# Four f chunks of the first two batches moved from twelve plain products into two seven-product pairs, with the loads of batches 1 to 3 reordered

## The chip, the core and the metric

The kernel runs on one core of a Trainium2 chip. The metric is device time in microseconds (us) of one execution. A core has a matrix engine (TensorE, PE in the profile; its weight loads are PEld), a vector engine (VectorE, DVE), a scalar engine (ScalarE, ACT), GpSimd (POOL, which here issues the input loads) and SyncE (SP, which issues the transposing DMAs and the stores). Each engine runs its own instructions in the order of the program and waits on semaphores. The matrix engine writes PSUM, which has eight banks; vector and scalar engine read it.

## What is computed

```python
# per batch b of 8 and head h of 12, sequence 448, head size 64
scores = q @ k.T / 8 - log(448)
attn   = sigmoid(scores)            # not a softmax
x      = concat_heads(attn @ v)     # 3584 tokens x 768
gate   = relu(x @ w_gate)           # w_gate, w_val: 768 x 1536
val    = x @ w_val
out    = (gate * val) @ w_out       # w_out: 1536 x 768
```

All products run in float16 with float32 accumulation.

## The kernel before

**Attention.** For each batch there are 21 score units: three groups g of four heads, seven chunks c each. A unit (`qk_unit`, L292) is four matmuls into two PSUM banks and two sigmoids on the scalar engine. `pv_group` (L300) then multiplies a whole group with v, 28 matmuls into two banks, and the vector engine scales the result into the tile `xT` (L184). Queries and keys must be transposed first. For batches 0 and 1 the matrix engine does that (`pe_transposes`, L195). From batch 2 on `dma_transposes` (L211) copies a group of k and q into the tile `rel` on the vector engine (L215) and SP issues one transposing DMA (L219).

**The feed-forward part.** Its unit is an f chunk, 128 of the 1536 columns of `w_gate` and `w_val`. For batches 0 and 1 it is done plainly by `gv` (L304): six gate matmuls and six value matmuls, a relu, a multiplication into `hT` (L327). Batch 0 is done in two halves of 256 and 192 tokens, batch 1 in one piece of 448. From batch 2 on two batches form a group, and `gv_pair` (L506) does two f chunks of both batches. There the two-by-two block product (gate and value columns against the two halves of the model dimension) is done in seven block products in place of eight, 42 matmuls of 448 columns. It needs sums of weight blocks (`gate_sums` L477 and `unit_sums` L481) and sums of activation blocks (`batch_sums` L500), all on the vector engine. The output product is done the same way for two token tiles (`down_pair` L423, after `token_sums` L409 and `weight_sums` L392, the latter four sums of blocks of `wo`); one token tile per group is done plainly (`down` L341, items "t").

**Order.** The program is written out by hand. The plain chunks stand in a queue; `ffn_mix` (L574) pops some of them and runs hooks at given places. Pairs, token tiles and output pairs stand in `work` (L659) and are taken by `next_work` (L675), which calls `prepare` for the next item's sums and runs a list of jobs beside its matmuls. Each batch is cut into stretches of score units (`cuts`), and after each stretch m come `mix[m]` plain chunks or one item of `work`. In batch 1 the mix is 3, 3, 3, 3, 3, 2, in batch 2 it is 2, 2, 1, 1, 1, 2 and then output pair 0 of group 0, in batch 3 it is 1, 1, 1 and then two items.

**PSUM.** `bank` (L76) hands out the eight banks in turn; a new tile waits for the readers of the last tile in its bank.

**Loads.** All input loads are issued by POOL, eight in flight. Through L160 they are issued as early as the queue allows: batch 0, the gate and value weights in five pieces, batch 1 between them. Those of batch 2 follow in batch 1. `hold(b, g)` (L645) is a copy of two elements on POOL out of a transposed tile: POOL issues nothing more until that transposing DMA has landed. In batch 1's last stretch `late_loads` (L652) holds for group 1 of batch 2, then loads v of batch 2 and `wo`; k, q and v of batch 3 follow in the first stretch of batch 2.

Of the kernel before, what the change touches and what calls it, by code (L numbers as in the profile page):

```python
# [17 lines left out]
def kernel(  # L18
# [10 lines left out]
    nc = tc.nc  # L29
# [6 lines left out]
    NCH = S // 64  # L36
    NDC = DM // P
    NFC = DF // P
    TW = 2 * NCH
    QCUT = 4  # L40
    HALVES = ((0, QCUT), (QCUT, NCH))
# [12 lines left out]
    PTp = ctx.enter_context(tc.tile_pool(name="PTp", bufs=11))  # L54
    xTp = ctx.enter_context(tc.tile_pool(name="xTp", bufs=3))
    hTp = ctx.enter_context(tc.tile_pool(name="hTp", bufs=1))
    ysbp = ctx.enter_context(tc.tile_pool(name="ysbp", bufs=4))
    gsbp = ctx.enter_context(tc.tile_pool(name="gsbp", bufs=6))
    first_sbuf = ExitStack()
    early = first_sbuf.enter_context(tc.tile_pool(name="early", bufs=1))  # L60
# [83 lines left out]
    def load_gv(f0, f1, which=(0, 1)):  # L144
        fs = slice(f0 * P, f1 * P)
        for i in which:
            wt, src = ((wg, moe_w_gate), (wv, moe_w_val))[i]
            nc.gpsimd.dma_start(wt[:, :, fs], src[:, fs].rearrange("(c p) f -> p c f", p=P))
# [4 lines left out]
    load_gv(2, 4)  # L153
    load_gv(4, 6)
    load(1, 0, 1, "kq")
    load_gv(6, 9)
    load(1, 1, 2, "kq")
    load_gv(9, 12)
    load_v(1)
    load(1, 2, 3, "kq")  # L160

# [206 lines left out]
    def open_late():  # L368
        first_sbuf.close()
        pool = ctx.enter_context(tc.tile_pool(name="late", bufs=1))  # L370
        late["T"] = pool.tile([P, 4, HF, HM], FP16, tag="T", name="T")
        late["X"] = pool.tile([P, 3, HD, S], FP16, tag="X", name="X")
        late["sums"] = ctx.enter_context(tc.tile_pool(name="sums", bufs=2))

    def sub(o, a, b):
        nc.vector.tensor_tensor(out=o, in0=a, in1=b, op=AOP.subtract)
# [114 lines left out]
    def batch_blocks(g, ks):  # L491
        x1, x2 = xT_tiles[2 * g], xT_tiles[2 * g + 1]
        lo, hi = slice(*ks), slice(HD + ks[0], HD + ks[1])
        return [late["X"][:, i, lo] for i in range(3)] + [x1[:, lo], x1[:, hi], x2[:, lo], x2[:, hi]]

    def batch_sums_t1(g):
        T1, _, _, B11, _, B12, _ = batch_blocks(g, (0, HD))
        sub(T1, B12, B11)

    def batch_sums(g, ks):  # L500
        T1, T2, T4, _, B21, B12, B22 = batch_blocks(g, ks)
        sub(B12, B22, B12)
        sub(T2, B22, T1)
        sub(T4, B21, T2)

    def gv_pair(g, f, beside, first_copy):  # L506
        x1, x2 = xT_tiles[2 * g], xT_tiles[2 * g + 1]
        T1, T2, T4 = (late["X"][:, i] for i in range(3))
        B11, B21, T3, B22 = x1[:, 0:HD], x1[:, HD:NDC], x2[:, 0:HD], x2[:, HD:NDC]
        b, c, a = ([bank(nm) for _ in range(2)] for nm in ("u", "g2", "g1"))  # L510
        later((6, 7, 4, 5, 2, 3))
        gs = [[gsbp.tile([P, S], FP32, tag="gsb", name="gsb") for _ in range(3)] for _ in range(2)]
        if g not in hT_tiles:
            hT_tiles[g] = hTp.tile([P, NFC, 2 * S], FP16, tag="hT", name="hT")
        h = hT_tiles[g]
        sets = []
        for u in range(2):
            us, fs = slice(u * P, (u + 1) * P), slice((f + u) * P, (f + u + 1) * P)
            S1, S2, S4 = (t[:, :, us] for t in sums[("w", g, f)])
            sets.append((  # L520
                wg[:, 0:HD, fs], wg[:, HD:NDC, fs], wv[:, HD:NDC, fs],
                S1, S2, wv[:, 0:HD, fs], S4,
            ))
        del sums[("w", g, f)]

        def product(ps, i, W, first=True):
            for u in range(2):
                products([(ps[u], S, HD, sets[u][i], W, first)])

        def copy(i, ps, by=nc.scalar.copy):  # L530
            for u in range(2):
                by(gs[u][i][:], ps[u][:, 0:S])  # L532

        def plus(i, ps):
            for u in range(2):
                nc.vector.tensor_tensor(  # L536
                    out=gs[u][i][:], in0=ps[u][:, 0:S], in1=gs[u][i][:], op=AOP.add
                )

        def gated(u, o, gate_sb, val):  # L540
            nc.vector.scalar_tensor_tensor(
                out=h[:, f + u, o : o + S], in0=gate_sb, scalar=0.0, in1=val, op0=AOP.max, op1=AOP.mult
            )

        product(b, 0, B11)
        copy(0, b, first_copy)
        product(c, 3, T1)
        copy(2, c)
        product(b, 4, T2, False)
        copy(1, b)  # L550
        beside()
        product(a, 1, B21)
        plus(0, a)
        product(b, 5, T3, False)
        plus(2, b)
        product(c, 6, B22, False)
        plus(1, c)
        product(b, 2, T4, False)
        for u in range(2):
            gated(u, 0, gs[u][0][:], b[u][:, 0:S])  # L560
        for u in range(2):
            gated(u, S, gs[u][1][:], gs[u][2][:])
# [7 lines left out]
    def push_first(half, fs, act_relu=True):  # L570
        c0, c1 = HALVES[half]
        push_gv(0, 64 * c0, 64 * (c1 - c0), fs, act_relu)
# [53 lines left out]
            if (i, u) in after:  # L626
                after[(i, u)]()
    slots[5].pv()
    push_first(1, range(0, 6))
    for f0 in range(6, 12, 2):  # L630
        for half in range(2):
            push_first(half, range(f0, f0 + 2))


    order = [(g, c) for g in range(NG) for c in range(NCH)]
# [1 line left out]
    def pv_finish(b):  # L637
        pv_group(b, NG - 1)
        if b < 2:
            push_gv(b, 0, S, range(NFC))  # L640

    first_psum.close()
    open_banks("ring1")
# [4 lines left out]
    def both(b, g):  # L648
        pe_transposes(b, g, 0)
        pe_transposes(b, g, 1)  # L650

    def late_loads():  # L652
        dma_transposes(2, 1)
        hold(2, 1)
        load_v(2)
        load_o()


    work = deque()  # L659

    def push_group(g):
        tail = [("t", g, 6)] + [("y", g, p) for p in range(3)]
        if g == 0:
            tail.insert(0, tail.pop(1))
        work.extend([("w", g, f) for f in range(0, NFC, 2) if g > 0] + tail)

    def prepare():
        if work:
# [6 lines left out]
    def next_work(jobs=(), alone=False, first_act=False):  # L675
        kind, g, i = work.popleft()

        def beside():
            for job in jobs:
                job()  # L680

        if kind == "y":
            down_pair(g, i, beside, prepare, not work, scaled_act if alone or first_act else scaled)
        elif kind == "w":
            gv_pair(g, i, lambda: (prepare(), beside()), nc.scalar.copy if alone else nc.vector.tensor_copy)
        else:
            beside()
            prepare()
            down(g, i)

    ffn_mix(1, [(1, lambda: both(1, 0))])
    for b in range(1, B):
# [6 lines left out]
        count = len(cuts) - 1  # L699
        hooks = {}  # L700
        if b == 1:
            mix = (3, 3, 3, 3, 3, 2)
            hooks = {
                1: [(1, lambda: both(1, 1))],
                3: [(1, lambda: both(1, 2))],
                4: [(3, lambda: dma_transposes(2, 0))],
                5: [(2, late_loads)],
            }
        elif b == 2:
            mix = (2, 2, 1, 1, 1, 2)  # L710
            hooks = {
                2: [(0, prepare)],
                4: [(0, lambda: weight_sums(0))],
                5: [(1, lambda: weight_sums(1)), (0, lambda: weight_sums(2))],
            }
            open_late()
        elif b == 3:
            mix = (1, 1, 1, 0, 0)
        else:
            mix = (0,) * count  # L720
        for m in range(count):
            jobs = []
            for i, (g, c) in enumerate(order[cuts[m] : cuts[m + 1]]):
# [7 lines left out]
                    else:  # L731
                        pv_group(b, pv_at[m][0])
                qk_unit(b, g, c)
            if m == 0 and b > 1:
                jobs.append(lambda: dma_transposes(b, 2))
            if b == 2 and m == count - 1:
                jobs.append(lambda: (dma_transposes(3, 0), dma_transposes(3, 1)))
            elif b == 3 and m == count - 1:
                jobs.append(lambda: (dma_transposes(4, 0), dma_transposes(4, 1)))
            elif 0 <= m - count + 2 and 3 < b < B - 1:  # L740
                jobs.append(lambda: dma_transposes(b + 1, m - count + 2))
            if b == 1:
                if m == 0:
                    load(2, 0, 1, "kq")
                    load(2, 1, 2, "kq")
                    load(2, 2, 3, "kq")
            elif m == 0 and b + 1 < B:
                if b == 3:
                    jobs.append(lambda: hold(3, 2))
                jobs.append(lambda: (load(b + 1, 0, 3, "kq"), load_v(b + 1)))  # L750
# [4 lines left out]
                jobs.append(lambda: batch_sums(b // 2 - 1, (1, HD)))  # L755
            if b == 2 and m == count - 1:
                ffn_mix(mix[m], hooks[m])
                next_work(jobs + [lambda: weight_sums(3)], first_act=True)
            elif mix[m]:
                for job in jobs:  # L760
                    job()
                ffn_mix(mix[m], hooks.get(m, ()))
            else:
                next_work(jobs)
            if b == 3 and m in (1, 3):
                for f in range(*((0, 8, 2), (8, NFC, 2))[m // 2]):
                    gate_sums(f, f + 2)
    pv_finish(B - 1)
    push_group(B // 2 - 1)
# [33 lines left out]
```

## Time and profile before

| what | value |
|---|---|
| three runs | 398.97, 397.96, 398.85 us; median 398.85 |
| the profiled execution | 399.14 us |
| its span, first to last instruction | 397.3 us |
| mean granted TensorE clock | 1.000 |
| from the first score unit of batch 1 to the last product before batch 2 | 33.83 to 64.25 us |
| batch 2, up to the first score unit of batch 3 | 64.25 to 101.36 us |
| engines busy in 33.83 to 64.25 (30.42 us) | PE 29.58, DVE 11.31, ACT 23.45 |
| engines busy in 64.25 to 101.30 (37.05 us) | PE 36.66, DVE 20.12, ACT 25.13 |

A timeline line gives the start in us, the stretch that the merged instructions cover, the engine, the line of the kernel, the operation, the tile written and the tiles read, the shape and the count; square brackets hold the idle time of the engine before them and what ended it. Instructions overlap at their ends. So the distance between two starts tells what one costs its engine, and the duration tells how long its result takes. DMA lines give the kilobytes written and the time from issue to landing.

### The profile page before, as it was taken

The numbers are of one execution on the slowest core, as the hardware profiler recorded it, in microseconds if no ns is written. First come the engines' busy times: TensorE is split into PE (matmuls) and PEld (weight loads), VectorE is DVE, ScalarE is ACT, GpSimd is POOL, SyncE is SP. The second block draws the span as 40 slices with busy tenths as digits, with TensorE's granted clock in tenths as the row PEclk, the third lists the DMA queues.
The fourth block names the chain that finished last, engine by engine and source line by source line (L and its number), as shares of the span: only waits on it lengthen the run. The fifth ranks groups of instructions, "written<-read, shape, count | busy, mean of one in ns | idle before, by whom it ended". The sixth has DMA issues, their size and how long they took to land.

```text
span 397.3 us, 8744 instructions
## 1 busy us (share of the span) xinstructions
PE 388.5 (98%) x3488; PEld 217.5 (55%) x3488; DVE 279.6 (70%) x539; ACT 223.2 (56%) x476; POOL 49.5 (12%) x73
## 2 busy tenths in 40 slices
PE   8999999999999999999999999999999999999995
PEld 3678686445455554554555555455455555555563
DVE  3453345358377889999758889999776779987662
ACT  5946768684785565655665455565566233543121
POOL 8643400700030300003000300000000000000000
PEclk9999999999999999999999999999999999999999
DMA  9999994999999893224945695222013320000135
GB/s 150 196 198 204 206 129 87 180 203 190 203 143 180 167 218 53 46 48 54 177 84 133 130 219 89 48 21 57 19 40 81 81 79 2 0 1 2 40 94 146
DMA packets 68953, 43.69 MB, mean 110 GB/s; under 512 B 35888, under 2 KB 65584, under 8 KB 68912
## 3 DMA queue, kind: packets, MB, share of 16 engines
q0 software_dynamic: 30736, 23.33, 39.2%
q1 hardware_dynamic: 37744, 19.34, 23.2%
q8 instruction: 27, 0.44, 0.4%
q10 hardware_dynamic: 432, 0.46, 0.4%
q14 instruction: 14, 0.11, 0.1%
HBM read 47.19 MB, written 11.01 MB: 146 GB/s over the span
## 4 chain that ended last, share of the span: by engine, by line
PE 84%; DMA 11%; POOL 2%; ACT 1%; issue 0%; DVE 0%; ACTq 0%; POOLq 0%; DVEq 0%
PE u L385 32%; PE g L385 15%; PE y L385 8%; PE qk_ps L232 7%; PE pv_ps L250 7%; PE g_ps L309 5%; PE v_ps L309 5%; DMA wg<-in_moe_w_gate_dram 4%; DMA v<-in_v_dram 3%; PE ya L346 3%; DMA q<-in_q_dram 2%; PE yb L346 1%; DMA qkT<-rel 1%; ACT PT L187 1%; POOL k L110 1%; POOL q L110 1%
## 5 line engine op out<-in xcount | busy, mean ns | idle before, releaser
L187 ACT ACTIVATE PT<-qk_ps 128x448 f16<-128x448 f32 (+3 forms) x318 | 150.5, 595 | 72.6 <-PE qk_ps L232 72.5
L385 PEld LDWEIGHTS <-S 128*128 128x128 f16 x540 | 52.8, 98 | 43.6
L536 DVE TENSOR_TENSOR gsb<-g,gsb 128x448 f32<-128x448 f32 x72 | 42.9, 625 | 14.6 <-PE g L385 14.1
L232 PE MATMUL qk_ps<-qkT 64*64 64x448 f16 (+2 forms) x756 | 49.9, 336 | 1.3 <-DVE qkT L206 0.5
L421 ACT ACTIVATE ysb<-u 128x384 f32<-128x384 f32 x27 | 13.4, 498 | 53.4 <-PE u L385 53.4
L327 DVE TENSOR_TENSOR hT<-gate_sb,v_ps 128x256 f16<-128x256 f32 (+2 forms) x36 | 16.2, 465 | 34.7 <-ACT gate_sb L318 22.3
L532 ACT COPY gsb<-u 128x448 f32<-128x448 f32 x48 | 25.7, 566 | 23.9 <-PE u L385 22.9
L250 PE MATMUL pv_ps<-PT,v 64*64 64x448 f16 (+2 forms) x756 | 37.7, 329 | 1.1 <-DMA v<-in_v_dram 0.8
L184 DVE TENSOR_SCALAR xT<-pv_ps 128x448 f16<-128x448 f32 (+2 forms) x53 | 27.9, 567 | 15.2 <-PE pv_ps L250 13.8
L385 PEld LDWEIGHTS <-hT 128*128 128x128 f16 x288 | 27.7, 98 | 19.8 <-issue 2.1
L232 PEld LDWEIGHTS <-qkT 64*64 64x64 f16 x756 | 20.0, 105 | 25.5 <-issue 16.3
L309 PE MATMUL v_ps<-xT,wv 128*128 128x256 f16 (+2 forms) x216 | 33.3, 290 | 0.3 <-DMA wv<-in_moe_w_val_dram 0.3
L309 PE MATMUL g_ps<-xT,wg 128*128 128x256 f16 (+2 forms) x216 | 33.5, 291 | 0.1
L385 PEld LDWEIGHTS <-wv 128*128 128x128 f16 x216 | 21.1, 98 | 19.7
L385 PEld LDWEIGHTS <-wg 128*128 128x128 f16 x216 | 20.3, 98 | 20.6 <-issue 3.0
L250 PEld LDWEIGHTS <-v 64*64 64x64 f16 x756 | 21.8, 107 | 12.8 <-DMA v<-in_v_dram 1.5
L385 PE MATMUL u<-T,hT 128*128 128x384 f16 x144 | 27.3, 326 | 0.0
L437 DVE SCALAR_TENSOR_TENSOR ysb<-y,ysb 128x384 f32<-128x384 f32 x24 | 13.4, 557 | 17.8 <-PE y L385 10.3
L309 PEld LDWEIGHTS <-wg 128*128 128x128 f16 x216 | 18.5, 98 | 11.5 <-issue 5.0
L110 POOL DMA_DIRECT2D k<-in_k_dram x14 | 10.9, 780 | 110.7 <-DVE rel L215 104.4
L309 PEld LDWEIGHTS <-wv 128*128 128x128 f16 x216 | 20.1, 98 | 7.9 <-DMA wv<-in_moe_w_val_dram 0.6
L385 PE MATMUL u<-xT,wg 128*128 128x448 f16 x108 | 23.5, 353 | 0.1
(69 smaller groups left out, 531.0 us busy)
## 6 DMA issues: line engine op xcount, KB each, us to landing
out_dram<-ysb SPq DMA_DIRECT2D x52, 192.0 KB, 3.0
k<-in_k_dram POOLq DMA_DIRECT2D x5, 672.0 KB, 11.7
q<-in_q_dram POOLq DMA_DIRECT2D x5, 672.0 KB, 14.9
v<-in_v_dram POOLq DMA_DIRECT2D x8, 336.0 KB, 15.4
v<-in_v_dram POOLq DMA_DIRECT2D x16, 168.0 KB, 15.2
k<-in_k_dram POOLq DMA_DIRECT2D x8, 224.0 KB, 10.4
wo<-in_moe_w_out_dram POOLq DMA_DIRECT2D x1, 1536.0 KB, 13.1
q<-in_q_dram POOLq DMA_DIRECT2D x6, 224.0 KB, 11.3
```

Source lines behind the costliest of these rows:

```text
L110: nc.gpsimd.dma_start(t16[:, xs, cs], rows_of(src, b)[:, xs, cs])
L184: nc.vector.tensor_scalar(out=xT, in0=src, scalar1=XSCALE, scalar2=None, op0=AOP.mult)
L187: nc.scalar.activation(PT_ap, ps_ap, AF.Sigmoid, bias=sig_bias, scale=qk_scale)
L232: nc.tensor.matmul(out_of(hh)[o : o + 64, :], qkT[rows, c, cols], qkT[rows, NCH + c0 : NCH + c1, cols], start=True, stop=True, tile_positi ...
L250: nc.tensor.matmul(ps[hh][64 * r : 64 * r + 64, 0:qn], v16[rows, 2 * g + hh, c * D : (c + 1) * D], pieces[c][rows, hh, :], start=(c == 0), ...
L309: nc.tensor.matmul(ps[-1][:, 0:qn], wt[:, dc, f * P : (f + 1) * P], xT_tiles[b][:, dc, q0 : q0 + qn], start=(dc == 0), stop=(dc == NDC - 1),)
L327: nc.vector.tensor_tensor(out=hT_tiles[g][:, f, o : o + qn], in0=gate_sb[:, 0:qn], in1=ps[1][:, 0:qn], op=AOP.mult,)
L346: nc.tensor.matmul(ps[:, 0 : m1 - m0], hT_tiles[g][:, f, t * P : (t + 1) * P], wo[:, f, m0:m1], start=(f == 0), stop=(f == NFC - 1),)
L385: nc.tensor.matmul(ps[:, 0:n], A[:, k_, :], W[:, k_, :], start=(first and k_ == 0), stop=(k_ == kn - 1), skip_group_check=True,)
L421: nc.scalar.activation(o, ps[:, 0:HM], AF.Copy, scale=OUT_SCALE)
L532: by(gs[u][i][:], ps[u][:, 0:S])
L536: nc.vector.tensor_tensor(out=gs[u][i][:], in0=ps[u][:, 0:S], in1=gs[u][i][:], op=AOP.add)
```

## The change

The last four f chunks (8 to 11) of batches 0 and 1 are no longer done by `gv`. They become two items "w" of `work` for group 0 (pair 8 and pair 10 below), done by `gv_pair` in batch 2 after the stretches m = 1 and m = 2. The constant `PAIR0 = 8` marks the first of them. A fourth activation sum gets a block of its own in the late tile `X` for group 0, since the plain chunks of batch 1 still read the block that the later groups overwrite. The buffers for output rows go from four to three. The relu of all plain chunks of batch 0 moves to the vector engine.

The mix of plain chunks becomes 2, 1, 2, 1, 2, 1 in batch 1 and 3, 0, 0, 1, 1, 0 in batch 2; a 0 takes an item of `work`, so batch 2 has pair 8, pair 10 and, after its last stretch, output pair 0. That output pair's first copy moves from the scalar to the vector engine. Its fourth weight sum, which stood beside its products, stands before them.

The weights of chunks 8 to 11 are loaded after a hold on the transposing DMA of batch 2's group 0 (`second_loads`), and ahead of the rest of batch 2's k, q and v. `wo` and batch 3's k and q come after a hold on batch 2's group 2 (`late_loads`), batch 3's v after a hold on batch 3's group 1.

```diff
...
-    ysbp = ctx.enter_context(tc.tile_pool(name="ysbp", bufs=4))
+    ysbp = ctx.enter_context(tc.tile_pool(name="ysbp", bufs=3))
...
     load(1, 0, 1, "kq")
-    load_gv(6, 9)
+    load_gv(6, 8)
     load(1, 1, 2, "kq")
-    load_gv(9, 12)
     load_v(1)
     load(1, 2, 3, "kq")
...
-        late["X"] = pool.tile([P, 3, HD, S], FP16, tag="X", name="X")
+        late["X"] = pool.tile([P, 4, HD, S], FP16, tag="X", name="X")
...
-    def batch_sums(g, ks):
-        T1, T2, T4, _, B21, B12, B22 = batch_blocks(g, ks)
-        sub(B12, B22, B12)
-        sub(T2, B22, T1)
-        sub(T4, B21, T2)
+    def batch_sums(g, ks, which=(3, 2, 4)):
+        T1, T2, T4, T3, _, B21, B12, B22 = batch_blocks(g, ks)
+        for i in which:
+            sub(*{2: (T2, B22, T1), 3: (T3, B22, B12), 4: (T4, B21, T2)}[i])
...
-    push_first(1, range(0, 6))
-    for f0 in range(6, 12, 2):
-        for half in range(2):
-            push_first(half, range(f0, f0 + 2))
+    push_first(1, range(0, 6), False)
+    for half in range(2):
+        push_first(half, range(6, PAIR0), False)
...
-            push_gv(b, 0, S, range(NFC))
+            push_gv(b, 0, S, range(PAIR0))
...
+    def second_loads():
+        dma_transposes(2, 0)
+        hold(2, 0)
+        load_gv(PAIR0, NFC)
+        load(2, 1, 2, "kq")
+        load(2, 2, 3, "kq")
+        load_v(2)
+
     def late_loads():
+        dma_transposes(2, 2)
+        hold(2, 2)
+        load_o()
+        load(3, 0, 3, "kq")
+
+    def first_sums():
+        batch_sums_t1(0)
+        batch_sums(0, (0, HD), (2,))
+
+    def other_sums():
+        batch_sums(0, (0, HD), (3, 4))
+
+    def gate_sums_then_prepare():
+        gate_sums(PAIR0, PAIR0 + 2)
+        prepare()
+
+    def gate_sums_then_transposes():
+        gate_sums(PAIR0 + 2, NFC)
         dma_transposes(2, 1)
-        hold(2, 1)
-        load_v(2)
-        load_o()
-
...
         if b == 1:
-            mix = (3, 3, 3, 3, 3, 2)
+            mix = (2, 1, 2, 1, 2, 1)
             hooks = {
                 1: [(1, lambda: both(1, 1))],
-                3: [(1, lambda: both(1, 2))],
-                4: [(3, lambda: dma_transposes(2, 0))],
-                5: [(2, late_loads)],
+                3: [(1, lambda: both(1, 2)), (0, second_loads)],
             }
         elif b == 2:
-            mix = (2, 2, 1, 1, 1, 2)
+            mix = (3, 0, 0, 1, 1, 0)
             hooks = {
-                2: [(0, prepare)],
-                4: [(0, lambda: weight_sums(0))],
-                5: [(1, lambda: weight_sums(1)), (0, lambda: weight_sums(2))],
+                0: [
+                    (3, first_sums),
+                    (2, gate_sums_then_prepare),
+                    (1, other_sums),
+                    (0, gate_sums_then_transposes),
+                ],
+                3: [(0, lambda: (prepare(), weight_sums(0)))],
+                4: [(1, lambda: weight_sums(1)), (0, lambda: weight_sums(2))],
+                5: [(0, lambda: weight_sums(3))],
             }
...
-                jobs.append(lambda: (dma_transposes(3, 0), dma_transposes(3, 1)))
+                jobs.append(lambda: (dma_transposes(3, 0), dma_transposes(3, 1), hold(3, 1), load_v(3)))
...
-                next_work(jobs + [lambda: weight_sums(3)], first_act=True)
+                next_work(jobs)
...
```

More of the change, by code (lines that the diff above doesn't have):

```diff
@@ L38 @@
     NFC = DF // P
+    PAIR0 = 8
     TW = 2 * NCH
@@ L493, in batch_blocks @@
         lo, hi = slice(*ks), slice(HD + ks[0], HD + ks[1])
-        return [late["X"][:, i, lo] for i in range(3)] + [x1[:, lo], x1[:, hi], x2[:, lo], x2[:, hi]]
+        T3 = (x2 if g > 0 else late["X"][:, 3])[:, lo]
+        return [late["X"][:, i, lo] for i in range(3)] + [T3, x1[:, lo], x1[:, hi], x2[:, lo], x2[:, hi]]
     def batch_sums_t1(g):
-        T1, _, _, B11, _, B12, _ = batch_blocks(g, (0, HD))
+        T1, _, _, _, B11, _, B12, _ = batch_blocks(g, (0, HD))
         sub(T1, B12, B11)
-    def batch_sums(g, ks):
-        T1, T2, T4, _, B21, B12, B22 = batch_blocks(g, ks)
-        sub(B12, B22, B12)
-        sub(T2, B22, T1)
-        sub(T4, B21, T2)
+    def batch_sums(g, ks, which=(3, 2, 4)):
+        T1, T2, T4, T3, _, B21, B12, B22 = batch_blocks(g, ks)
+        for i in which:
+            sub(*{2: (T2, B22, T1), 3: (T3, B22, B12), 4: (T4, B21, T2)}[i])
     def gv_pair(g, f, beside, first_copy):
@@ L508, in gv_pair @@
         T1, T2, T4 = (late["X"][:, i] for i in range(3))
-        B11, B21, T3, B22 = x1[:, 0:HD], x1[:, HD:NDC], x2[:, 0:HD], x2[:, HD:NDC]
+        B11, B21, B22 = x1[:, 0:HD], x1[:, HD:NDC], x2[:, HD:NDC]
+        T3 = x2[:, 0:HD] if g > 0 else late["X"][:, 3]
         b, c, a = ([bank(nm) for _ in range(2)] for nm in ("u", "g2", "g1"))
@@ L664, in push_group @@
             tail.insert(0, tail.pop(1))
-        work.extend([("w", g, f) for f in range(0, NFC, 2) if g > 0] + tail)
+        work.extend([("w", g, f) for f in range(0 if g > 0 else PAIR0, NFC, 2)] + tail)
     def prepare():
@@ L684, in next_work @@
         elif kind == "w":
-            gv_pair(g, i, lambda: (prepare(), beside()), nc.scalar.copy if alone else nc.vector.tensor_copy)
+            gv_pair(g, i, lambda: ((g > 0 or i < NFC - 2) and prepare(), beside()), nc.scalar.copy if alone else nc.vector.tensor_copy)
         else:
@@ L733 @@
                 qk_unit(b, g, c)
-            if m == 0 and b > 1:
+            if m == 0 and b > 2:
                 jobs.append(lambda: dma_transposes(b, 2))
+            if b == 2 and m == 1:
+                jobs.append(late_loads)
             if b == 2 and m == count - 1:
-                jobs.append(lambda: (dma_transposes(3, 0), dma_transposes(3, 1)))
+                jobs.append(lambda: (dma_transposes(3, 0), dma_transposes(3, 1), hold(3, 1), load_v(3)))
             elif b == 3 and m == count - 1:
@@ L744 @@
                     load(2, 0, 1, "kq")
-                    load(2, 1, 2, "kq")
-                    load(2, 2, 3, "kq")
-            elif m == 0 and b + 1 < B:
+            elif m == 0 and 2 < b < B - 1:
                 if b == 3:
@@ L765 @@
             if b == 3 and m in (1, 3):
-                for f in range(*((0, 8, 2), (8, NFC, 2))[m // 2]):
+                for f in range(*((0, 4, 2), (4, PAIR0, 2))[m // 2]):
                     gate_sums(f, f + 2)
```

## The prediction

> **What bounds the kernel now.** I read the page's busy shares and its chain of work first, then the timeline of PE by stage, then those of POOL and DVE.
>
> ```profile
> PE 388.5 (98%) x3488; PEld 217.5 (55%) x3488; DVE 279.6 (70%) x539; ACT 223.2 (56%) x476; POOL 49.5 (12%) x73
> PE 84%; DMA 11%; POOL 2%; ACT 1%; issue 0%; DVE 0%; ACTq 0%; POOLq 0%; DVEq 0%
> ```
>
> PE is the bound. The chain leaves it only for the loads of the first 49 us. So a change gains what it takes off PE's stream, and loses what it adds in PE waits; nothing later has slack to give a wait back.
>
> ```profile
> 36.02 0.66 PE L309 MATMUL v_ps<-xT,wv 128*128 128x192 f16 x6
> 36.51 0.66 PE L309 MATMUL g_ps<-xT,wg 128*128 128x192 f16 x6
> ...
> 43.38 0.83 PE L309 MATMUL g_ps<-xT,wg 128*128 128x256 f16 x6
> 44.05 0.82 PE L309 MATMUL v_ps<-xT,wv 128*128 128x256 f16 x6
> 44.70 0.66 PE L309 MATMUL g_ps<-xT,wg 128*128 128x192 f16 x6
> ...
> 47.18 0.35 PE L250 MATMUL pv_ps<-PT,v 64*64 64x448 f16 x2
> 47.83 0.37 PE L250 MATMUL pv_ps<-PT,v 64*64 64x448 f16 x1 [0.29 <-DMA v<-in_v_dram]
> 48.69 1.51 PE L250 MATMUL pv_ps<-PT,v 64*64 64x448 f16 x25 [0.49 <-DMA v<-in_v_dram]
> ```
>
> Starts six matmuls apart give the cost: 0.66 us at 256 columns, 0.50 at 192. At 448 columns six take 1.135 (L309 starts at 67.61 and 68.75). The last rows are the one wait on a load after the start: batch 1's first pv takes from 47.18 to 49.85 in place of 1.32 us, 1.35 lost.
>
> **PE's own sum.** Removed: four chunks at 12 x 256 (1.31 each), four at 12 x 192 (0.995), four at 12 x 448 (2.27), together 18.3. Added: two pairs of seven products of 1.135, 15.9. That is -2.4. Batch 1's v now stands behind 1,536 KB less of weights; at 200 KB/us it lands 7.7 us earlier, at 41, and PE wants it at 42.7: -1.35. ACT does not take over in batch 1: 21 units of two sigmoids at 0.43 each are 18.2 us, PE keeps 21.2.
>
> **The loads of chunks 8 to 11.** They now wait for a transposing DMA, and that waits for DVE's `rel` copies at the end of batch 1's fourth stretch. Up to there PE has, from 33.83: 13 units (0.25 each), five chunk halves of 0.995 and one of 1.31, two sets of transposes (0.87 each), one pv: 12.6, and 0.4 of bank waits on ACT, so 46.8; the copies end at 48.1. What follows the hold is in POOL's timeline and in the DMA issues of the same stretch:
>
> ```profile
> 109.32 0.17 POOL L646 COPY gate<-qkT 1x2 f16<-1x2 f16 x1 [31.70 <-DMA qkT<-rel]
> 109.86 0.86 POOL L110 DMA_DIRECT2D k<-in_k_dram  x1 [0.36 <-issue]
> ```
> ```profile
> k<-in_k_dram POOLq DMA_DIRECT2D x1, 672.0 KB, 7.1
> q<-in_q_dram POOLq DMA_DIRECT2D x1, 672.0 KB, 9.6
> ```
>
> So 0.5 us from hold to issue, 7.1 to the landing of 672 KB, 3.4 for each 672 KB behind. Transposing DMAs took 3.9 to 5.6 on quiet queues; the first two took 5.1 and 5.6, I take 4.6. The hold passes at 52.8, `wg` (768 KB) lands at 60.9, `wv` at 64.9. DVE wants both for `gate_sums`: PE has, after 46.8, 12 units, chunks of 1.31 and twice 1.0 and two pv, 9.0, then the first 448-column chunk, 2.27, then its multiplication: 58.9. **DVE waits 6 us**, and the multiplications that free the banks of the next two plain chunks stand behind it.
>
> [...]
>
> **From there to output pair 0.** DVE's distances between starts:
>
> ```profile
> 94.19 0.62 DVE L327 TENSOR_TENSOR hT<-gate_sb,v_ps 128x448 f16<-128x448 f32 x1
> 94.73 1.35 DVE L376 TENSOR_TENSOR T<-wo 128x2304 f16<-128x2304 f16 x1
> 96.00 0.39 DVE L215 COPY rel<-k 128x896 f16<-128x896 f16 x1
> ...
> 138.47 0.56 DVE L487 TENSOR_TENSOR S<-S,wg 128x768 f16<-128x768 f16 x1
> 138.94 0.55 DVE L376 TENSOR_TENSOR S<-wg,S 128x768 f16<-128x768 f16 x1
> ```
>
> A multiplication is 0.54, a weight sum T of `wo` 1.27, a 768-column sum 0.47 (0.59 when the next needs it), a `rel` copy 0.30; a 1,344-column sum is 0.85 long. Behind the wait stand: one gate difference and three sums 2.1, multiplication 0.54, two activation sums 1.54, multiplication 0.6. Then, at +4.8, the bank of the last plain chunk is free and pair 8 can go on: half a product, one product, and at +6.6 its third; five more, +12.3. Units and a pv 2.2, pair 10 7.95, units and a plain chunk 2.96: +25.4. Now DVE is late by itself. Multiplication 0.7, token sums 2.15, two T 2.54, xT 1.1, multiplication 0.54, two T 2.54 and output pair 0's first copy 0.6 stand ahead of that pair's third product, 10.2 where PE needs 7.15. Before, the last T stood later and ACT made the copy. The first T waits 1.0 more, since `wo` starts behind the hold on group 2: `rel` ends at +9.1, transposing 4.05, issue 0.5, 3.7 to the first bytes, 2,304 KB at 196 KB/us: +29.2, wanted at +28.2. Together 36.5: output pair 0's third product starts at 64.9 + 36.5 = 101.4. Before it was
>
> ```profile
> 95.87 1.14 PE L385 MATMUL u<-T,S 128*128 128x384 f16 x6
> ...
> 101.36 0.57 PE L232 MATMUL qk_ps<-qkT 64*64 64x448 f16 x8 [0.45 <-DMA qkT<-rel]
> ```
>
> Batch 3's scores need `rel` after the first copy (0.6) and a transposing DMA (4.6): 106.6 against 101.36, **+5.2**, all of PE's savings counted in it.
>
> **Batch 3's v.** It now waits for the second transposing DMA. SP issues that 2.3 after the first (96.75 and 99.06 before) and it takes 4.15: lands at 108.4, POOL issues at 109.0. 672 KB then take 7.1, or 9.9 beside a transposing DMA, as the k load issued at 133.62; the one for group 2 is issued at 110.2. Landing: 116.1 to 118.9. PE wants it 8.5 after 106.6 (109.88 before), 115.1. A wait of 1.0 to 3.8; with no reason to prefer an end I take 2.4.
>
> **Three row buffers.** Only the last group has output pairs back to back. There a pair's second row tile waits for the stores of the last pair's first one, written 2 us into the pair.
>
> ```profile
> out_dram<-ysb SPq DMA_DIRECT2D x52, 192.0 KB, 3.0
> ```
>
> At 3.0 PE loses 0 to 0.2 a pair. The stores issued there at 378.93 and 379.44 landed at 381.90 and 383.71; at that PE would lose 1.5. Bounds 0 to 1.9; I take 0.3, near the median. The other edits (relu on DVE in batch 1, 0.27 to 0.34 each beside a DVE that is busy 11.3 of 30.4 us; fewer gate differences in batch 3) lie under PE; uncovered they would cost at most their sum, about 2.8, and save at most 1.
>
> **Sum.** 5.2 + 2.4 + 0.3 = +7.9, on the profiled 399.14: **407.0 us**. The median of the three runs is 0.3 below that execution, which is inside what I can resolve. With transposing 3.9, v 1.0 and stores 0 it is 404.6; with 5.6, 3.8 and 1.9 it is 411.0.
>
> **Rivals.** A, *the loads come in time, faster*: PE keeps its -2.4 and -1.35 and loses only DVE's 3 us before output pair 0, which it would have to hide too: 395.4 to 398.4, say 397. It decides where `wv` lands by 59.9 and v of batch 3 by 115; for it, ACT and DVE have room on average; against it, the chain of copy, transposing DMA, hold and 1,536 KB is 16.8 us by rows and PE reaches the reader in 10.8. B, *the weights come in time, but DVE and batch 3's v do not*: -3.75 + 3.0 - 0.4 + 2.4 + 0.3, 400.7. C, *the waits cost more than their length*, 413. The granted clock is 1.000 all through and PE's longest idle time after 50 us is 0.45; now it would idle 4.2 us at one stretch, which no row shows. [...]
>
> **Chances.** Forecast 0.69, A 0.12, B 0.13, C 0.06. The range 400.0 to 411.5 leaves out A, part of C and the low edge of B. About 0.3% is what a measurement here can tell from no change: faster by more 0.12, within it 0.05 (B's low edge), slower 0.83.
>
> **What would show it.** Right: a DVE wait on DMA wv of about 6 us near 59, PE idle about 4 us near 63 behind it, PE waiting for DVE before output pair 0's third product, a PE wait on DMA v near 115, L309 without PE's wait on v near 47. Wrong: `gate_sums` without a DMA wait, or batch 3's first score unit before 102.

## The result, and the profile after

The changed kernel takes 410.65 us, median of six executions (408.37 to 414.27), against 398.61 (397.96 to 398.97): 1.0311 times as long, interval 1.0259 to 1.0363. The profiled execution took 412.68 us, the second slowest of the six; its span is 410.7 against 397.3.

From the page: PE's busy time, the chain by engine, and PE's granted clock in 40 slices.

```profile
PE 394.8 (96%) x3428; PEld 215.8 (53%) x3428; DVE 298.0 (73%) x572; ACT 220.3 (54%) x461; POOL 50.3 (12%) x75
PEclk9999998997898999999999999999999999999998
PE 77%; DMA 13%; DVE 3%; ACT 3%; issue 2%; POOL 1%; ACTq 0%; DVEq 0%; POOLq 0%; SPq 0%
```

PE has 60 matmuls fewer and is busy 6.3 us longer. That can't be work; the second row shows what it is. Before, the clock was full in all slices. Here slices 7, 10, 11 and 13 (10.3 us each: 62 to 72, 92 to 113 and 123 to 133) show 8, 7, 8 and 8. In the chain, DMA and DVE have taken shares that PE had.

PE's timeline holds three places where it waits, and matmuls behind them that take up to twice their time (six of 384 columns 1.14, six of 448 1.31 before):

```profile
66.75 0.38 PE L232 MATMUL qk_ps<-qkT 64*64 64x448 f16 x3 [1.66 <-DVE hT L327]
68.82 1.28 PE L385 MATMUL u<-xT,wg 128*128 128x448 f16 x3 [0.61 <-DVE hT L327]
...
98.44 1.86 PE L232 MATMUL qk_ps<-qkT 64*64 64x448 f16 x12 [3.28 <-DVE xT L184]
100.24 2.10 PE L385 MATMUL u<-wo,hT 128*128 128x384 f16 x6
104.05 1.52 PE L385 MATMUL u<-T,S 128*128 128x384 f16 x6
109.40 0.57 PE L232 MATMUL qk_ps<-qkT 64*64 64x448 f16 x8
...
118.92 0.37 PE L250 MATMUL pv_ps<-PT,v 64*64 64x448 f16 x1 [0.46 <-DMA v<-in_v_dram]
120.87 1.87 PE L250 MATMUL pv_ps<-PT,v 64*64 64x448 f16 x25 [1.58 <-DMA v<-in_v_dram]
123.43 2.21 PE L309 MATMUL g_ps<-xT,wg 128*128 128x448 f16 x6
```

The brackets of the first two places name the vector engine. Its own rows there tell what it waited for:

```profile
63.96 0.56 DVE L376 TENSOR_TENSOR wv<-wg,wv 128x768 f16<-128x768 f16 x1 [3.36 <-DMA wv<-in_moe_w_val_dram]
96.50 1.36 DVE L376 TENSOR_TENSOR T<-wo 128x2304 f16<-128x2304 f16 x1 [2.69 <-DMA wo<-in_moe_w_out_dram]
```

So three loads are late: the weights of chunks 8 to 11, `wo`, and v of batch 3. A window row gives start and end, length, busy time of PE, PEld, DVE, ACT and POOL, PE's granted clock, the DMA share and GB/s:

```profile
67.00:79.00 12.00, 11.39 (x85) 5.51 (x86) 11.65 (x23) 4.49 (x10) 0.48 (x1) 0.86 1.00 149
98.00:106.00 8.00, 7.55 (x34) 3.49 (x34) 6.93 (x11) 3.61 (x8) 0.00 (x0) 0.57 0.49 82
118.00:126.00 8.00, 5.96 (x49) 2.47 (x46) 2.71 (x5) 4.42 (x11) 3.24 (x6) 0.79 0.79 85
```

Length times the missing clock is 1.7, 3.4 and 1.7 us: some 6.8 of the 13.4 us that the span grew by are not waiting but matmuls at half clock behind a wait. What they cost is less, since at full clock PE would in part have waited instead. At the first place the wait for the vector engine lasts until 68.82 whatever the clock; only from there to the end of the slow stretch, at 70.7, is PE held up, by 0.9. At the second, where the vector engine is behind `wo`, it comes to about 0.2, at the third to 1.6 (both by the run with v of batch 3 early, below). That is about 2.7 us, an estimate from these rows.

In the six executions the mean clock was 0.981, 0.995, 0.981, 0.992, 0.987 and 0.987, with spans of 410.7, 407.0, 411.3, 406.5, 409.0 and 408.5. The spans lie 4.8 apart, span times clock (402.9 to 405.0) 2.1: more than half of the scatter goes with the clock.

By place: batch 3's first score unit comes at 109.40 in place of 101.36 (+8.0), the first product of the next plain token tile at 127.87 in place of 115.43 (+12.4), the end 13.4 later. So 1.0 us is added behind 128 us, 0.6 of it by two gaps of 0.28 in the last output pairs.

### The profile page after: what moved, and what is told of

It is laid out like the page before. It is cut to its first block, busy times and chain, and to the rows that moved or that the text cites. A ratio compares the mean times of both kernels' runs of the same rounds, so it can differ in the third digit from the quotient of the medians.

```text
span 410.7 us, 8648 instructions
## 1 busy us (share of the span) xinstructions
PE 394.8 (96%) x3428; PEld 215.8 (53%) x3428; DVE 298.0 (73%) x572; ACT 220.3 (54%) x461; POOL 50.3 (12%) x75
## 4 chain that ended last, share of the span: by engine, by line
PE 77%; DMA 13%; DVE 3%; ACT 3%; issue 2%; POOL 1%; ACTq 0%; DVEq 0%; POOLq 0%; SPq 0%
PE u L385 30%; PE g L385 15%; PE y L385 7%; PE qk_ps L232 7%; PE pv_ps L250 6%; DMA wo<-in_moe_w_out_dram 4%; DMA qkT<-rel 3%; PE g_ps L309 3%; PE ya L346 3%; DMA wv<-in_moe_w_val_dram 2%; ACT PT L187 2%; PE v_ps L309 2%; DMA v<-in_v_dram 2%; DMA out_dram<-ysb 1%; PE yb L346 1%
## 5 line engine op out<-in xcount | busy, mean ns | idle before, releaser
L385 PEld LDWEIGHTS <-S 128*128 128x128 f16 x576 | 57.1, 99 | 48.4 <-issue 2.6
L537 DVE TENSOR_TENSOR gsb<-g,gsb 128x448 f32<-128x448 f32 x80 | 47.6, 624 | 17.1 <-PE g L385 16.6
L385 PEld LDWEIGHTS <-wg 128*128 128x128 f16 x240 | 22.6, 98 | 24.2 <-issue 5.1
L385 PEld LDWEIGHTS <-wv 128*128 128x128 f16 x240 | 23.5, 98 | 21.9
L385 PE MATMUL u<-X,wv 128*128 128x448 f16 x132 | 28.6, 352 | 0.0
L437 DVE SCALAR_TENSOR_TENSOR ysb<-y,ysb 128x384 f32<-128x384 f32 x24 | 13.4, 557 | 19.5 <-PE y L385 11.9
L385 PE MATMUL g<-X,S 128*128 128x448 f16 x120 | 26.4, 356 | 0.0
L385 PE MATMUL u<-X,S 128*128 128x448 f16 x120 | 26.0, 352 | 0.0
L385 PE MATMUL g<-xT,wg 128*128 128x448 f16 x120 | 26.0, 352 | 0.0
L385 PE MATMUL g<-xT,S 128*128 128x448 f16 x120 | 26.0, 352 | 0.0
L537 DVE TENSOR_TENSOR gsb<-u,gsb 128x448 f32<-128x448 f32 x40 | 23.9, 625 | 0.5 <-issue 0.3
## 6 DMA issues: line engine op xcount, KB each, us to landing
k<-in_k_dram POOLq DMA_DIRECT2D x8, 224.0 KB, 10.3
```

Of the source, the lines that this page charges most:

```text
L385: nc.tensor.matmul(ps[:, 0:n], A[:, k_, :], W[:, k_, :], start=(first and k_ == 0), stop=(k_ == kn - 1), skip_group_check=True,)
L437: nc.vector.scalar_tensor_tensor(out=o, in0=ps[:, 0:HM], scalar=OUT_SCALE, in1=o, op0=AOP.mult, op1=AOP.add)
L537: nc.vector.tensor_tensor(out=gs[u][i][:], in0=ps[u][:, 0:S], in1=gs[u][i][:], op=AOP.add)
```

## The experiments

My theory after the result: each of the three loads is a wait on the path, and a drop of the clock follows it. The main rival: the vector engine, which has all the new sums, is late by itself, whatever the loads do. The medians stand against 410.65 for the changed kernel and 398.2 to 398.4 for the kernel before, which ran beside each.

**Weights ahead of the hold.**

```diff
         dma_transposes(2, 0)
+        load_gv(PAIR0, NFC)
         hold(2, 0)
-        load_gv(PAIR0, NFC)
```

> The gate and value weights of chunks 8 to 11 are issued ahead of the hold on batch 2's group 0, all else as in the changed kernel. First theory (three late loads, each a wait on the path, and two of them followed by a stretch of lower granted clock): they are issued near 37 and land near 52, as 1,536 KB at about 200 KB/us behind q of batch 2 at 44.3; gate_sums has no DMA wait, the 1.66 and 0.61 us of PE idle near 67 go, and the time falls by about 2.3 to 408.3. Rival (vector engine: the sums for two pairs and for output pair 0 make it late by themselves, whatever the loads do): the 2.3 us come back as a longer PE wait before output pair 0, and the time falls by less than 0.8. Second rival (only the clock loss is dear, the waits are hidden by it): less than 1 too, with the mean clock as low as 0.981 to 0.995.

406.21 us, 4.4 less. `gate_sums` has no wait left, pair 8 starts at 64.51 and runs through at full clock. That is about twice the waits that went (2.3 us), since the slow stretch behind them (1.7) went as well. The rival for this place falls. What is left before output pair 0:

```profile
92.06 0.35 PE L232 MATMUL qk_ps<-qkT 64*64 64x448 f16 x1 [1.52 <-DVE xT L184]
94.59 2.13 PE L385 MATMUL y<-T,S 128*128 128x384 f16 x6
```

**`wo` early.**

```diff
     def second_loads():
...
         load_v(2)
+        load_o()
...
     def late_loads():
...
         hold(2, 2)
-        load_o()
```

> wo is issued behind v of batch 2 instead of behind the hold on batch 2's group 2. First theory: wo lands near 85 (2,304 KB at 196 KB/us behind v of batch 2, which landed at 71.8 in the changed kernel), the first T of wo has no wait (2.69 us in the changed kernel), PE's idle time of 3.28 us before output pair 0 falls below 1, the granted clock in that stretch stays at 1.00 in place of 0.57, and the time falls by 2.7 for the wait and 2 to 3 for the clock, to about 405.5. Rival (vector engine late by itself): two T and the first copy still make PE wait about 3 us there, the time falls by 1 at most. Rival (a wait costs its length and no more): the time falls by 2.7, to 408.

418.98 us, 8.3 more than the changed kernel. My theory failed here. `wo` landed at 89.05 and the first T had no wait, as expected. But the transposing DMAs of batch 2's groups 1 and 2 were now issued, at 69.94 and 76.94, while `wo` was in flight. The view of the tile `qkT` from 60 to 90 us gives them from issue to landing, in the changed kernel and then with `wo` early:

```profile
DMA to landing us min/median/max: 4.0/4.6/5.3
```
```profile
DMA to landing us min/median/max: 13.1/14.5/15.8
```

The first landed at 85.76, after the first piece of `wo` (82.59), the second at 90.08, 1.0 after the second piece. PE stood still for them:

```profile
85.81 0.96 PE L232 MATMUL qk_ps<-qkT 64*64 64x448 f16 x8 [6.78 <-DMA qkT<-rel]
```

So the hold in front of `wo` is not what is wrong with the order: it keeps a long load out of the way of a transposing DMA. The load is late because the transposing DMA ahead of it is late.

**v of batch 3 early.**

```diff
         load(3, 0, 3, "kq")
+        load_v(3)
...
-                jobs.append(lambda: (dma_transposes(3, 0), dma_transposes(3, 1), hold(3, 1), load_v(3)))
+                jobs.append(lambda: (dma_transposes(3, 0), dma_transposes(3, 1)))
```

> v of batch 3 is issued behind its k and q and no longer behind the hold on batch 3's group 1. First theory: it lands near 104, the two PE waits on it (0.46 and 1.58 us near 120) and the slow matmuls after them (1.32 and 2.21 in place of 0.72 and 1.31) go: the time falls by 2.5 for the waits and 1.4 for the clock, to about 406.8. Rival (a wait costs its length and no more): falls by 2.5 at most, to 408.2. Rival (transfer hidden anyway, PE held by the scalar or vector engine at that place): less than 1.

406.73 us, 3.9 less, as the theory said: the pv at 116.45 has no wait, and no slow stretch follows. In this run PE also waits 1.40 us before output pair 0 and 1.87 before its third product, and there the clock stays at 1.00:

```profile
97.16 0.35 PE L232 MATMUL qk_ps<-qkT 64*64 64x448 f16 x1 [1.40 <-DVE xT L184]
102.49 1.14 PE L385 MATMUL u<-T,S 128*128 128x384 f16 x6 [1.87 <-DVE ysb L416]
107.93 0.57 PE L232 MATMUL qk_ps<-qkT 64*64 64x448 f16 x8 [0.40 <-DMA qkT<-rel]
```

Up to here this program differs from the changed kernel only in loads behind q of batch 3. So this is the place of the 3.28 us once more, with `wo` awaited for 0.81 us in place of 2.69 (0.78 in the run with the first copy back on the scalar engine, further down). From the plain chunk before output pair 0 to batch 3's first score unit PE takes 14.6 us here and 16.7 in the changed kernel's profile. Of the 2.1 between them, `wo` explains 1.9. By this one pair of profiles the 3.4 us of missing clock cost about 0.2: at full clock PE waits for the vector engine and the transposing DMA instead. For v the two profiles agree with the theory. From the last 25 products of pv to the plain token tile PE takes 1.6 us less, besides the waits that went.

**All three edits.**

> The three edits together: weights ahead of the hold, wo behind v of batch 2, v of batch 3 behind its k and q. First theory: the three add up, 2.3 + 5.2 + 3.9, to about 399.3, granted clock above 0.998, and what is left against the kernel before is the vector engine's lateness before output pair 0 less PE's own saving of 2.4. Rival (vector engine late by itself): PE still waits 3 us or more before output pair 0 and the time stays above 403. Third possibility, for which the seven-product pairs would have to be worth their whole saving: 396, faster than the kernel before.

411.35 us. Neither theory foresaw it, but after the second run it follows: the first transposing DMA takes 15.2 us (66.72 to 81.88), PE waits 8.5. The sum of the single effects, 418.98 - 4.4 - 3.9 = 410.7, comes near it. For the first and the third edit without the second there is no measurement.

**One wait by itself, in the kernel before**: the third weight sum of `wo` made five times, then twice.

```diff
-                5: [(1, lambda: weight_sums(1)), (0, lambda: weight_sums(2))],
+                5: [(1, lambda: weight_sums(1)), (0, lambda: [weight_sums(2) for _ in range(5)])],
```

> The kernel before, with the third weight sum of wo computed five times in place of once (the same values again): the vector engine is 4 x 1.27 = 5.1 us later at output pair 0 and at the rel copies of batch 3, which PE has to wait for. Nothing else is changed, so the price of one long PE wait is measured by itself. If a wait costs its length: 398.4 + 5.1 = 403.5, granted clock 1.000 as before apart from the idle time. If a long wait is followed by slow matmuls: 405 to 407, matmuls of twice the normal distance behind the wait and a mean clock below 0.996. If there was slack in the vector engine there: under 402.

403.62 us, 5.25 more, mean clock 0.989 to 0.995.

```profile
100.34 2.10 PE L385 MATMUL u<-T,hT 128*128 128x384 f16 x6 [3.73 <-DVE T L376]
102.23 1.56 PE L385 MATMUL y<-wo,S 128*128 128x384 f16 x6
103.74 1.14 PE L385 MATMUL u<-T,hT 128*128 128x384 f16 x6
```

Of the 5.1 us of vector work, 1.4 was hidden by slack. The wait of 3.73 costs 1.89 - 0.98 and 1.51 - 0.98 on top, from one start to the next: 1.4 us. The slow clock is shown without any late load. The total fell short of the 405 to 407 that I gave, because I had not seen the slack.

> The kernel before, with the third weight sum of wo computed twice in place of once. With four more of them, 5.1 us of vector work gave one PE idle time of 3.73 us with 3 us at a granted clock of 0.50 behind it, and the time rose by 5.25. One more is 1.27 us: PE may wait up to 1.7 us for the transposing DMA of batch 3 (0.45 before). If a short wait is not followed by a slow clock: 398.4 plus 1.3 at most, 399.7, and a mean clock of 0.999 to 1.000. If the slow clock follows any wait of more than a microsecond: 400.5 or more.

399.11 us (1.0018, 1.0008 to 1.0028). One wait of 1.00 us, and 0.19 in place of 0.45 at batch 3's first score unit; clock 0.997 to 1.000, time 0.74 more. So this short wait cost its length and no more.

**Three row buffers in the kernel before**, nothing else:

```diff
-    ysbp = ctx.enter_context(tc.tile_pool(name="ysbp", bufs=4))
+    ysbp = ctx.enter_context(tc.tile_pool(name="ysbp", bufs=3))
```

> The kernel before with three row buffers in place of four, the one part of the change that acts at the end. The changed kernel's PE has two gaps of about 0.25 us in its last output pairs. If they are the row buffers: 0.3 to 0.6 slower than the kernel before, about 398.9, with the same two gaps, and the first 350 us as before. If they are not: 398.4 and no gaps. If stores at times take as long as the slowest in the kernel before (4.27 us): up to 1.9 slower.

400.33 us, 2.0 more (1.0047, 1.0032 to 1.0062): the upper bound, not the small cost that I expected.

```profile
384.28 1.14 PE L385 MATMUL u<-T,hT 128*128 128x384 f16 x6 [1.74 <-ACT ysb L421]
```

The scalar engine waited 3.21 us there for the stores issued at 378.36 and 378.87, which took 3.1 and 4.4 us. In the profile of the changed kernel the same stores, issued at 391.75 and 392.26, took 2.6 and 2.8, and PE's two gaps were 0.28 each. Why a store at that place takes 2.8 us in one kernel and 4.4 in the other is open.

**The vector engine's order.** First the first copy of output pair 0 back on the scalar engine and the fourth weight sum beside its products, nothing else:

```diff
-                5: [(0, lambda: weight_sums(3))],
+                5: [],
-                next_work(jobs)
+                next_work(jobs + [lambda: weight_sums(3)], first_act=True)
```

> The changed kernel with output pair 0's first copy back on the scalar engine and the fourth weight sum beside its products again; the three late loads stay. If the vector engine by itself is a part of the loss before output pair 0: its list gets 1.27 and 0.5 us shorter, the rel copies of batch 3 come at the earliest behind the fourth sum as before, so the wait before the third product (1.5 to 1.9) goes while the 3.3 in front of the pair stays: 1.5 to 2 less than the changed kernel, about 409, and less still if the slow clock behind it gets shorter. Rival (wo alone sets that place): no change, 410.6.

410.15 us (408.65 to 410.49), 0.5 less, which the scatter of the changed kernel does not let me tell from nothing. The wait before the third product fell to 0.70 us, but the late v of batch 3 took the rest: its waits were 0.52, 0.77 and 1.79 there. Then the same with the weights ahead of the hold, and the first weight sum of `wo` behind the scaling of batch 2's group 1:

```diff
-                3: [(0, lambda: (prepare(), weight_sums(0)))],
-                4: [(1, lambda: weight_sums(1)), (0, lambda: weight_sums(2))],
+                3: [(0, prepare)],
+                4: [(1, lambda: (weight_sums(0), weight_sums(1))), (0, lambda: weight_sums(2))],
```

> The changed kernel with the weights of chunks 8 to 11 ahead of the hold (406.2 alone), the first copy back on the scalar engine with the fourth weight sum beside the products, and the first weight sum of wo behind the scaling of batch 2's group 1, so that no bank is held by a wait for wo. v of batch 3 stays late. If the vector engine's order is what is left before output pair 0: PE's 1.5 and 0.7 us of idle time there go, with the clock of 0.72 behind them, and batch 3's first score unit comes at 99 to 100 in place of 102.4 (101.4 in the kernel before), the time at 402.5 to 404 with the wait for v still in it. Rival (vector work is too much in whatever order): the first score unit stays at 101.5 or later, 405 to 406.

404.49 us (403.00 to 408.18), between the ranges of the theory and of the rival. The profile is that of the slowest execution. The 1.52 us are gone, and 1.34 and 2.02 have come in their place, at full clock; the first score unit of batch 3 comes at 102.43. That is the rival's side of 101.5. But the vector engine is not full there:

```profile
97.72 0.39 DVE L215 COPY rel<-q 128x896 f16<-128x896 f16 x1 [2.29 <-DMA q<-in_q_dram]
```

It waits for q of batch 3, which stands in the queue behind `wo`, behind the hold. One cause would explain both: the transposing DMA of batch 2's group 2 is issued too late. The next run moves it, with all the rest.

**Everything at once**: weights ahead of the hold; the two `rel` copies of batch 2's groups 1 and 2 moved ahead of pair 8, so that `wo` is issued at 72.1 in place of 79.8; v of batch 3 behind its k and q; the vector engine's order as above with the second weight sum behind the last multiplication; four row buffers, since the fourth activation sum of group 0 lies where the fourth weight sum will be.

```diff
-        late["X"] = pool.tile([P, 4, HD, S], FP16, tag="X", name="X")
+        late["X"] = pool.tile([P, 3, HD, S], FP16, tag="X", name="X")
+        late["T3"] = late["T"][:, 3].rearrange("p x y -> p (x y)")[:, 0 : HD * S].rearrange(
+            "p (x y) -> p x y", y=S
+        )
...
-                    (1, other_sums),
-                    (0, gate_sums_then_transposes),
+                    (1, lambda: dma_transposes(2, 1)),
+                    (0, late_loads),
+                    (0, lambda: gate_sums(PAIR0 + 2, NFC)),
...
-                jobs.append(late_loads)
+                jobs.append(other_sums)
```

> The pairs kept, everything that the runs so far showed as dear taken out. Weights of chunks 8 to 11 ahead of the hold; the rel copies and transposing DMAs of batch 2's groups 1 and 2 some 3 to 4 us earlier, before pair 8, and the sums of activations beside it; so wo, k, q and v of batch 3 are issued near 71 in place of 75 to 80, in one row; first copy of output pair 0 on the scalar engine, the fourth weight sum beside its products, the other three behind the scaling and the last multiplication; four row buffers, since the fourth activation sum of group 0 takes the place of the weight sum that is not yet made. Theory (loads, vector engine's order, row buffers and the clock behind the waits were all of the loss): q of batch 3 lands near 93 in place of 97.7, batch 3's first score unit at 99.5 to 100.5 in place of 101.4 in the kernel before, no PE wait on v, clock 0.998 or more, time 396.5 to 398, faster than the kernel before. Rival (vector engine full from 57 to 76 and again from 86 to 96, so that every gap closed there opens another): first score unit at 101.5 to 103, 399 to 401, slower than the kernel before.

398.82 us, median of 11, against 398.23: 1.001 (1.0001 to 1.0019). All that the change lost is back, and it is not faster. As the run joins several edits, their single shares are not shown.

```profile
94.26 1.14 PE L388 MATMUL u<-T,S 128*128 128x384 f16 x6 [0.83 <-ACT ysb L424]
99.91 0.57 PE L232 MATMUL qk_ps<-qkT 64*64 64x448 f16 x8 [0.58 <-DMA qkT<-rel]
```

Apart from 0.2 us near 54 these are its only gaps. q of batch 3 lands at 94.56, its first score unit comes at 99.91, as the theory said, 1.45 before the kernel before. Of the 3.75 us in PE's own sum (2.4 of matmuls, 1.35 of the wait for v), 1.0 goes to these two gaps net of the 0.45 before; 0.8 to bank waits in batch 1, where the scalar engine has little room (in the changed kernel it is busy 7.61 us of the 8 from 50 to 58); the rest, about 0.5, I have not placed. At the end the lead is 1.1 by the two profiles. But the profiled execution of the kernel before had a longer span (397.3) than most of its others (396.3 to 396.7), and this kernel spends 2.2 to 3.2 us outside its span where that one spends 1.8. The medians of the spans are 396.4 here and 396.5 there. So nothing is left of the lead within the span, and the 0.6 us between the median times lies outside it, which the profile does not show.

## Why the prediction was right, and where it was not

The time lay in the range and the direction was right: late loads behind holds. But part of its nearness is luck. Pair 8's third product starts at 71.42, where the sum has 64.9 + 6.6 = 71.5: the vector engine's wait ended at 63.96 and not at 64.9, and the 0.9 us of half clock behind it, which the sum does not have, made up for that.

- **PE's own sum**: right. Batch 1, up to the first score unit of batch 2, takes 20.5 us in place of 30.4, 9.9 less; the sum said 9.2 for eight chunk halves and 1.35 for v, 10.55. The wait for v is gone, as given. The step "ACT does not take over in batch 1" was 0.6 off: it is busy 7.61 us of the 8 from 50 to 58, and I take it that banks wait for it.
- **Weights of chunks 8 to 11**: the mechanism right, the wait 3.36 in place of 6. The transposing DMA took 4.1 in place of 4.6, `wg` and `wv` landed 6.9 and 10.7 after the first issue in place of 7.6 and 11.6, and the vector engine reached the reader 1.7 later. PE stood still for 1.66 and 0.61 us behind it, not for 4. As the first experiment shows it was worth 4.4, more than the length of these waits.
- **Output pair 0**: its third product starts at 104.05 in place of 101.4. In the sum `wo` lands at 64.9 + 29.2 = 94.1, in the profile at 96.5: the transposing DMA ahead of the hold took 5.3 in place of 4.05, POOL took 1.3 from the hold to the issue in place of 0.5, and 2,304 KB took 16.6 from the first issue in place of 15.5. So the wait for it was 2.69 in place of 1.0; two other runs with the same order had 0.81 and 0.78, near the 1.0. The vector engine's own share was near what was given: with `wo` early PE still waits 0.50, 0.18 and 1.87 there, 2.55 of 3.05. In the changed kernel's profile the wait stands in front of the pair, not at its third product, as I had put it.
- **Batch 3's first score unit**: 109.40 in place of 106.6, by the same delay of `wo`; 107.93 in the run where `wo` was awaited for 0.81 us.
- **v of batch 3**: PE starts on it at 118.09, the last piece lands at 120.83: 2.7, where 2.4 was taken. Worth 3.9 with the clock behind it.
- **Three row buffers**: 0.6 in the profile where 0.3 was taken, within 0 to 1.9; alone in the kernel before, 2.0.
- **Rival C, the waits cost more than their length**, is the step that was wrong, a term put at nothing. I gave it 0.06 and weighed it for one wait; its 413 was my estimate, which no row gives. The half clock came three times. The median lies nearer to C's 413 than to 407.0, and the profiled execution, 412.68, lies on it; the forecast holds because its range reached up to 411.5. By the estimate above the half clock was worth 2.7 of the 5.6 us by which that execution passes 407.0; `wo`, which landed 2.4 later than in the sum, weighs about as much. What the executions would take without the half clock is not shown. If all the missing clock is taken off, which is too much, they stand at 404.9 to 406.9, with the time outside the span; with 2.7 off, the profiled one stands at 410.0.

Where the clock was low it was 0.50. In the changed kernel's trace it drops at 67.27, 97.99 and 121.88, for 3.41, 6.83 and 3.41 us. The length of a wait alone does not tell whether a drop comes: waits of 3.28 and 3.73 us had one in or behind them, but so had one of 1.66, or 1.52 and 0.19 (the run with the weights ahead of the hold), while 1.40 and 1.87 (v of batch 3 early) and 2.02 (weights ahead of the hold and the vector engine's order) had none. Nor does the idle time just ahead: in the 3.41 us before each of the three drops PE was busy for 1.75, 0.60 and 1.38; with v of batch 3 early it was busy for 1.13 of the 3.00 us from 100.16 to 103.16, and the clock stayed at 1.00. What decides it is not shown.

## What to carry to other kernels

Before a load is put behind a hold, write down the whole row that then stands in front of it: the copy, the transposing DMA, the hold, the issue, the bytes ahead; and compare its end with the time at which the last reader, not PE, wants it. A wait of the matrix engine of 1.00 us cost its length here. Some longer ones, of 1.66 to 3.73 us, had matmuls at a clock of 0.50 behind them, and others, of 1.40 to 2.02, had not. The slow matmuls cost 1.4 us on top of a wait of 3.73 where nothing else held the engine up, and about 0.2 where the vector engine was late anyway. And a saving in matmuls is worth only what the slowest of the loads, the vector engine and the scalar engine leaves of it: here the 3.75 us of PE's own sum came to nothing that can be measured.

## What the runs showed that I had not expected

- Transposing DMAs took longer beside a long load. With `wo` early the two issued while it was in flight took 15.8 and 13.1 us, where the same two took 4.0 and 5.3 in the changed kernel. In the changed kernel the one issued at 113.23 beside v of batch 3 took 9.0; the one issued at 136.99, 1.6 us before the last load in flight landed, took 4.1.
- A slow stretch of the matrix engine in the changed kernel was at 0.50 of the clock throughout and lasted 3.41 or 6.83 us. It did not begin with the end of the wait: 0.5 us after it at 67.27 and 1.0 at 121.88, and 0.5 before it at 97.99, where the wait ended at 98.44.
